# Interleaving the k products of the first two x chunks, with x1 loaded ahead of wk0 and the transposes and later loads held back

## The chip, the cores and the metric

The kernel runs on one core of one Trainium2 chip. The metric is the device time of one execution in microseconds (us), as a median over several executions. PE is the matrix engine, DVE the vector engine, ACT the scalar engine, SP the engine that issues most of the loads. To "turn" a chunk is to transpose it on PE, by products with an identity matrix. "SP's queue" and "ACT's queue" are the DMA issues of those two engines.

## The reference, cut to what matters

The whole computation is a gated mix of a linear-attention block and an MLP mixer over 2048 rows of 640 numbers. Only its first stage matters here: k = x @ wk, of which the rest of the attention block is made.

```python
qkv = (x @ wqkv) ...            # wqkv is 640 x 1920; its middle third is wk
phi = lambda t: jnp.where(t > 0, t + 1, jnp.exp(t)) + 1e-6
pq, pk = phi(q), phi(k)
g = sigmoid((x * gate_w).sum(-1, keepdims=True))   # the gate, computed as a 641st column of k
...                              # attention, mixer, g * a + (1 - g) * b
```

## The kernel before

x is cut into 16 chunks of 128 rows, wk into 5 pieces of 128 rows (160 KB each). A product for k needs x transposed (xT). Chunks 0 and 1 are loaded plain and turned on PE; chunks 2 to 15 are transposed by DMA. The issue order is: SP's queue x0, wk1, wk3, wk4, then the transposes; ACT's queue gate_w, wk0, x1, wk2.

```python
    load_x(0, 1)
    aq.dma_start(g5[:], gate_w.rearrange("(c p) -> c p", p=P))
    load_wk(sp, 1)
    load_wk(aq, 0)
    load_x(1, 2, aq)
    load_wk(sp, 3)
    load_wk(aq, 2)
    load_wk(sp, 4)
    for c0, c1 in ((2, 3), (3, 4), (4, 6), (6, 8), (8, 12), (12, 16)):
        load_xT(c0, c1)
    sp.dma_start(wq_sb, wqkv_v[:, :, 0:D])
    load_x(2, 8)
    load_x(8, 16)
    ...
```

The k products of one chunk are 5 pieces times 2 halves. A filler (`warmup`) is a product of ones that nobody reads; it only keeps PE busy.

```python
    def k_mm(pt, c, dcs, first=0, last=DC - 1):
        for dc in dcs:
            for hf in range(2):
                n = HD + hf
                nc.tensor.matmul(pt[:, hf, 0:n], lhsT=xT[:, dc, c * P:(c + 1) * P],
                                 rhs=wk_sb[:, dc, hf * HD:hf * HD + n], start=(dc == first), stop=(dc == last))

    warm = pair()
    one = nc.const_aps.tensor(1.0, (P, TS), BF16)

    def warmup(n, w=TS):
        for i in range(n):
            nc.tensor.matmul(warm[:, 1, 0:w], lhsT=one[:, 0:P], rhs=one[:, 0:w], start=True, stop=True)
    nc.vector.memset(g5z[:], 0.0)
    nc.vector.tensor_copy(g5z[0:DC, :], g5[:])
    warmup(5)
    warmup(1, 3 * P)
    kp = pair()
    turns = [(pair(), a, b) for a, b in ((0, 2), (2, DC))]

    def turn(c):
        for pt, a, b in turns:
            ptb = pt[:, 0, :].bitcast(BF16) if c else pt[:, 0, :]
            for dc in range(a, b):
                dst, src = ptb[:, (dc - a) * P:(dc - a + 1) * P], x_sb[:, c, dc * P:(dc + 1) * P]
                if c:
                    nc.tensor.transpose(dst, src, ident[:])
                else:
                    nc.tensor.matmul(dst, lhsT=src, rhs=ident[:], start=True, stop=True)
            if c == 0 and b == DC:
                nc.tensor.matmul(pt[:, 1, 0:DC], lhsT=g5z[:], rhs=ident[:, 0:DC], start=True, stop=True)
            nc.vector.tensor_copy(xT[:, a:b, c * P:(c + 1) * P],
                                  ptb[:, 0:(b - a) * P].rearrange("p (c s) -> p c s", c=b - a))
            if c == 0 and b == DC:
                nc.vector.tensor_copy(wk_sb[:, :, D], pt[:, 1, 0:DC])

    turn(0)
    warmup(1, TS)
    for n, dc in enumerate(k0_order):
        if n == 3:
            turn(1)
        elif 1 <= n < 3:
            warmup(1, 2 * P)
        k_mm(kp, 0, (dc,), first=k0_order[0], last=k0_order[-1])
    k_evac(kp, 0)
    for c in range(1, NCH):
        pt = pair()
        k_mm(pt, c, range(DC))
        k_evac(pt, c)
```

After k come q, the attention sums and the mixer, all of it PE work in program order, with nothing of the change in it.

## Time and profile before

| | before |
|---|---|
| median of 3 runs | 264.6 us (264.48 to 264.68) |
| span of the profiled run | 262.6 us |
| PE busy | 257.9 us, 98% |
| k chunk 2 starts | 8.35 us |
| k chunk 4 starts / its transpose landed | 11.07 / 9.72 us |
| k chunk 8 starts / its transpose landed | 16.52 / 16.44 us |
| first product of the next large group (`x_sb`,`pk`) | 49.01 us |

The landing times here and below are the times at which the last of the 16 partial signals of a load arrived, read from the trace. The starts are those of the 160 k products in order. These come from the packed traces product by product and signal by signal, and most of them stand in no view shown here.

First the page of before: the span, the busy line, the busy tenths of PE and of the DMA engines in 40 slices of 6.6 us, and the head of the chain that ended last.

```profile
span 262.6 us, 4246 instructions
...
PE 257.9 (98%) x1719; PEld 160.0 (61%) x1738; DVE 142.7 (54%) x282; ACT 82.7 (31%) x123; POOL 20.2 (8%) x65
...
PE   8999999999999999999999999999999999999995
...
DMA  7999987016682566600132000051100051100011
...
PE 98%; issue 0%; DVE 0%
```

PE is all that counts: its own work is 98% of the chain. Next, the chain in order of time in before, cut to the pieces from 4.69 to 27.6 us (start, length, what):

```profile
4.69 0.03 issue
4.72 0.43 PE pp L186
5.14 0.21 PE pp L199
5.36 0.47 PE pp L186 x2
5.83 0.11 PE pp L199
5.94 0.27 PE pp L186 x2
6.21 0.32 PE pp L214 x5
6.53 21.05 PE pp L186 x154
```

The one of these pieces that is not PE work is 30 ns of "issue" at 4.69 us (the second half of the first product has just been held up by the gate column); from there PE works on without a wait. The stretch from 3.2 us in windows, before (length, then busy time of PE, PE weight loads, DVE, ACT, POOL with counts, the granted clock, the DMA share, GB/s; the DMA share adds up the times of packets over 16 engines and can exceed 1):

```profile
3.20:6.00 2.80, 2.77 (x16) 1.67 (x15) 0.97 (x3) 0.82 (x1) 1.42 (x5) 1.00 1.14 336
6.00:8.30 2.30, 2.30 (x21) 1.69 (x20) 0.87 (x3) 0.77 (x2) 0.00 (x0) 1.00 1.16 233
```

PE is busy 2.77 of 2.80 us and then 2.30 of 2.30 us. The timeline of PE of before shows what it does (start, length, engine, line, operation, operands, shape, count):

```profile
5.15 0.68 PE L186 MATMUL pp<-wk_sb,xT 128*128 128x320 bf16 x2
5.66 0.27 PE L199 MATMUL pp<-const-bfloat16-1.0 128*128 128x256 bf16 x1
5.77 0.44 PE L186 MATMUL pp<-wk_sb,xT 128*128 128x320 bf16 x2
6.08 0.45 PE L214 MATMUL pp<-ident,x_sb 128*128 128x128 bf16 x5
6.44 5.75 PE L186 MATMUL pp<-wk_sb,xT 128*128 128x320 bf16 x41
```

A product of 320 columns follows the last after 267 ns up to about 5.6 us, and after 136 ns later. The Trainium skill, "TensorE: Matmul & The Clock Gate", Part 1, says that PE passes half of its clock pulses until it has been busy for a window of about 3.4 us, and that the moment varies between runs since the window runs free. This agrees: at the page's half rate of 1.2 GHz, 320 columns would take 267 ns (an estimate from its figure), and the trace has 267 ns. The granted clock reads 1.00 all the same, so it does not show this half rate; the spacing of the products does.

Last, the transposes in SP's timeline of before (start, length of issuing all six), and DVE's two copies of the first turn in its own timeline:

```profile
2.65 14.00 SPq L122 DMA_TRANSPOSE xT<-in_A_x_dram  x6
```

```profile
3.69 0.89 DVE L219 CAST xT<-pp 128x256 bf16<-128x256 f32 x2 [1.28 <-PE pp L216]
```

The transposes are issued from 2.65 us on. DVE's first copy starts at 3.69 us, released by the second turn product (L216).

### The profile page before, as it was taken

How to read it: one execution, taken by the hardware profiler on the slowest of the kernel's cores; microseconds unless marked ns; L12 is line 12 of the kernel's file. 1: busy time of each engine (PE TensorE's matmuls, PEld its weight loads, DVE VectorE, ACT ScalarE, POOL GpSimd, SP SyncE). 2: the span in 40 equal slices, each digit the busy share in tenths (PEclk: the TensorE clock that was granted, in tenths of full speed). 3: DMA queues.
4: the chain of work that ended last, by engine and by line, in shares of the span. 5: the costliest groups of instructions: out<-in, count | busy, mean ns of one | idle time of the engine just before them, and what ended most of it. 6: DMA issues, size and time to landing. Idle time of an engine off the chain costs nothing.

```text
span 262.6 us, 4246 instructions
## 1 busy us (share of the span) xinstructions
PE 257.9 (98%) x1719; PEld 160.0 (61%) x1738; DVE 142.7 (54%) x282; ACT 82.7 (31%) x123; POOL 20.2 (8%) x65
## 2 busy tenths in 40 slices
PE   8999999999999999999999999999999999999995
PEld 4777555788755644555577555567565577555553
DVE  2788778899947998955403464413356223112132
ACT  1555554321166236522502222412131332142200
POOL 5000050012210040001000001000001000000000
DMA  7999987016682566600132000051100051100011
GB/s 204 197 171 379 364 248 304 0 27 125 125 99 58 111 121 167 235 0 2 25 75 77 25 0 2 0 100 52 50 0 2 1 100 52 50 0 2 0 50 50
DMA packets 45757, 23.98 MB, mean 91 GB/s; under 512 B 35114, under 2 KB 44970, under 8 KB 45738
## 3 DMA queue, kind: packets, MB, share of 16 engines
q1 hardware_dynamic: 45296, 23.22, 35.1%
q10 hardware_dynamic: 442, 0.49, 0.5%
q8 instruction: 13, 0.21, 0.4%
q14 instruction: 6, 0.05, 0.1%
HBM read 12.21 MB, written 2.62 MB: 56 GB/s over the span
## 4 chain that ended last, share of the span: by engine, by line
PE 98%; issue 0%; DVE 0%
PE pp L500 22%; PE pp L467 21%; PE pp L186 9%; PE pp L315 8%; PE pp L451 8%; PE pp L420 8%; PE pp L349 8%; PE pp L243 8%; PE pp L199 1%; PE pp L387 1%; PE pp L475 1%; PE pp L509 1%; PE pp L368 1%; PE pp L258 0%; PE pp L216 0%
## 5 line engine op out<-in xcount | busy, mean ns | idle before, releaser
L467 PE MATMUL pp<-lnxT,w_sb 128*128 128x512 bf16 x249 | 59.8, 379 | 0.6
L500 PE MATMUL pp<-w_sb,h 128*128 128x384 bf16 (+3 forms) x414 | 57.6, 299 | 0.2 <-issue 0.2
L469 ACT ACTIVATE h<-pp 128x1024 bf16<-128x1024 f32 (+1 forms) x28 | 26.9, 961 | 82.2 <-PE pp L467 82.2
L500 PEld LDWEIGHTS <-h 128*128 128x128 bf16 x416 | 38.3, 98 | 19.3 <-issue 1.1
L467 PEld LDWEIGHTS <-w_sb 128*128 128x128 bf16 x260 | 25.4, 98 | 26.8
L514 DVE SCALAR_TENSOR_TENSOR oc<-pp,omg,x 128x640 bf16<-128x640 f32 (+2 forms) x20 | 14.4, 748 | 45.1 <-ACT h2x L478 21.3
L454 DVE SCALAR_TENSOR_TENSOR x<-pp,gate,x 128x640 f32<-128x640 f32 x16 | 13.9, 868 | 29.4 <-PE pp L451 29.4
L178 ACT ACTIVATE e<-pp 128x640 bf16<-128x640 f32 (+1 forms) x26 | 21.5, 826 | 9.6 <-PE pp L243 9.6
L451 PE MATMUL pp<-m_sb,pqT 128*128 128x320 bf16 x160 | 24.3, 299 | 0.0
L420 PE MATMUL pp<-w_sb,hsT 128*128 128x320 bf16 x160 | 23.9, 299 | 0.0
L423 DVE TENSOR_TENSOR x<-pp,x_sb 128x640 f32<-128x640 f32 x16 | 13.1, 820 | 19.7 <-PE pp L420 19.7
L186 PE MATMUL pp<-wk_sb,xT 128*128 128x320 bf16 (+1 forms) x160 | 23.1, 303 | 0.0
L315 PE MATMUL pp<-x_sb,pk 128*128 128x320 bf16 (+1 forms) x160 | 22.0, 300 | 0.0
L243 PE MATMUL pp<-xT,hsT 128*128 128x512 bf16 x98 | 21.6, 379 | 0.1
L315 PEld LDWEIGHTS <-pk 128*128 128x128 bf16 x160 | 18.8, 117 | 3.2
L420 PEld LDWEIGHTS <-hsT 128*128 128x128 bf16 x160 | 15.7, 98 | 8.2
L451 PEld LDWEIGHTS <-pqT 128*128 128x128 bf16 x160 | 15.7, 98 | 7.7
L186 PEld LDWEIGHTS <-xT 128*128 128x128 bf16 x160 | 15.7, 99 | 6.5 <-DVE xT L219 0.2
L349 PE MATMUL pp<-lnxT,w_sb 128*128 128x512 bf16 x76 | 17.9, 379 | 0.2
L243 PEld LDWEIGHTS <-hsT 128*128 128x128 bf16 x100 | 11.8, 118 | 9.7
L285 POOL TENSOR_SCALAR rstd<-mv 128x4 f32<-128x4 f32 (+1 forms) x11 | 3.4, 312 | 153.6 <-DVE mv L291 153.6
L180 DVE SCALAR_TENSOR_TENSOR pk<-pp,e 128x640 bf16<-128x640 f32 x16 | 13.2, 825 | 1.7
(76 smaller groups left out, 189.9 us busy)
## 6 DMA issues: line engine op xcount, KB each, us to landing
out_dram<-oc SPq DMA_DIRECT2D x14, 160.0 KB, 1.8
w_sb<-in_B_w_dram SPq DMA_DIRECT2D x1, 2160.0 KB, 8.4
w_sb<-in_B_w_dram SPq DMA_DIRECT2D x1, 2080.0 KB, 9.9
x_sb<-in_A_x_dram SPq DMA_DIRECT2D x1, 1280.0 KB
x_sb<-in_A_x_dram SPq DMA_DIRECT2D x1, 960.0 KB, 7.4
wo_sb<-in_A_wo_dram SPq DMA_DIRECT2D x6, 160.0 KB, 7.8
hsT<-in_A_wqkv_dram SPq DMA_DIRECT2D x1, 800.0 KB, 5.1
m_sb<-in_A_wqkv_dram SPq DMA_DIRECT2D x1, 800.0 KB, 12.0
```

Of the source, the lines that this page charges most:

```text
L178: nc.scalar.activation(ev, src, ACT.Exp)
L186: nc.tensor.matmul(pt[:, hf, 0:n], lhsT=xT[:, dc, c * P:(c + 1) * P], rhs=wk_sb[:, dc, hf * HD:hf * HD + n], start=(dc == first), stop=(dc ...
L243: nc.tensor.matmul(pt[:, t % 2, :], lhsT=wq_sb[:, dc, :].rearrange("p (m j) -> p j m", j=DC)[:, j], rhs=xT[:, dc, t * TS:(t + 1) * TS], st ...
L315: nc.tensor.matmul(pt[:, hf, 0:HD + hf], lhsT=w, rhs=x_sb[:, c, hf * HD:(hf + 1) * HD + hf], start=(c == 0), stop=(c == NCH - 1))
L349: nc.tensor.matmul(pt[:, i, :], lhsT=w, rhs=lnxT[t][:, dc, :], start=(dc == 0), stop=(dc == DC - 1))
L420: nc.tensor.matmul(pt[:, hf, 0:HD], lhsT=hsT[:, fc, 2 + c * P:2 + (c + 1) * P], rhs=w2_sb[:, fc, hf * HD:(hf + 1) * HD], start=(fc == 0), ...
L451: nc.tensor.matmul(pt[:, hf, 0:HD], lhsT=pqT[:, j, c * P:(c + 1) * P], rhs=m_sb[:, j, hf * HD:(hf + 1) * HD], start=(j == 0), stop=(j == D ...
L454: nc.vector.scalar_tensor_tensor(x1, pt[:, :, 0:HD], gate[:, c:c + 1], x1, op0=ALU.mult, op1=ALU.add)
L467: nc.tensor.matmul(pt[:, k, :], lhsT=w3_sb[:, dc, fc * P:(fc + 1) * P], rhs=lnT[:, dc, :], start=(dc == 0), stop=(dc == DC - 1))
L469: nc.scalar.activation(h2[:, 2 * i * TS:(2 * i + n) * TS], pt[:].rearrange("p h e -> p (h e)")[:, 0:n * TS], ACT.Gelu_apprx_tanh)
L500: nc.tensor.matmul(dst, lhsT=st[t]["h2"][:, fc * TS + cc * P:fc * TS + (cc + 1) * P], rhs=w4_sb[:, fc, a:b], start=start and fc == 0, stop ...
L514: nc.vector.scalar_tensor_tensor(oc[:, a:b], src, omg[:, c:c + 1], st[t]["x1"][cc][:, a:b], op0=ALU.mult, op1=ALU.add)
```

## The change

The intent: use each wk piece for both first chunks as soon as it lands, so that nothing of chunk 1 is left when the last piece has come. For this x1 is loaded ahead of wk0 on ACT's queue, chunk 1 is turned early by plain products, and ACT copies it out. The gate column is copied ahead of the larger copy. The transposes and everything behind them are held back by a memset on the first transposed column, so that they don't take DMA time from the wk pieces.

```diff
--- before.py
+++ after.py
@@ -127,24 +127,26 @@
     load_x(0, 1)
     aq.dma_start(g5[:], gate_w.rearrange("(c p) -> c p", p=P))
     load_wk(sp, 1)
-    load_wk(aq, 0)
     load_x(1, 2, aq)
     load_wk(sp, 3)
+    load_wk(aq, 0)
+    load_wk(sp, 4)
     load_wk(aq, 2)
-    load_wk(sp, 4)
-    for c0, c1 in ((2, 3), (3, 4), (4, 6), (6, 8), (8, 12), (12, 16)):
-        load_xT(c0, c1)
-    sp.dma_start(wq_sb, wqkv_v[:, :, 0:D])
-    load_x(2, 8)
-    load_x(8, 16)
-    sp.dma_start(wv_sb[:], wqkv_v[:, :, 2 * D:3 * D])
-    sp.dma_start(w1_sb[:], B_w1.rearrange("(c p) f -> p c f", p=P))
-    for g in range(NG):
-        sp.dma_start(wo_sb[:, g, :], A_wo[row0[g]:row0[g] + P, :])
-    for g in range(4):
-        sp.dma_start(w2_sb[:, g, :], B_w2[CG * g:CG * g + P, :])
-        sp.dma_start(w2_sb[32 * g:32 * (g + 1), 4, :], B_w2[CG * g + P:CG * (g + 1), :])
-    sp.dma_start(w3_sb[:], B_w3.rearrange("(c p) f -> p c f", p=P))
+
+    def late_loads():
+        for c0, c1 in ((2, 3), (3, 4), (4, 6), (6, 8), (8, 12), (12, 16)):
+            load_xT(c0, c1)
+        sp.dma_start(wq_sb, wqkv_v[:, :, 0:D])
+        load_x(2, 8)
+        load_x(8, 16)
+        sp.dma_start(wv_sb[:], wqkv_v[:, :, 2 * D:3 * D])
+        sp.dma_start(w1_sb[:], B_w1.rearrange("(c p) f -> p c f", p=P))
+        for g in range(NG):
+            sp.dma_start(wo_sb[:, g, :], A_wo[row0[g]:row0[g] + P, :])
+        for g in range(4):
+            sp.dma_start(w2_sb[:, g, :], B_w2[CG * g:CG * g + P, :])
+            sp.dma_start(w2_sb[32 * g:32 * (g + 1), 4, :], B_w2[CG * g + P:CG * (g + 1), :])
+        sp.dma_start(w3_sb[:], B_w3.rearrange("(c p) f -> p c f", p=P))
 
 
     nc.gpsimd.memset(mhalf[:], -0.5)
[cut: the copies of w1x are moved behind late_loads()]
@@ -190,47 +189,48 @@
         nc.scalar.copy(ylog[:, c:c + 1], pt[:, 1, HD:HD + 1])
         phi(pk[:, c, :].rearrange("p (h e) -> p h e", h=2), pt[:, :, 0:HD], D)
 
-    k0_order = (1, 0, 3, 4, 2)
     warm = pair()
     one = nc.const_aps.tensor(1.0, (P, TS), BF16)
 
-    def warmup(n, w=TS):
+    def warmup(n, w=TS, pt=warm):
         for i in range(n):
-            nc.tensor.matmul(warm[:, 1, 0:w], lhsT=one[:, 0:P], rhs=one[:, 0:w], start=True, stop=True)
+            nc.tensor.matmul(pt[:, 1, 0:w], lhsT=one[:, 0:P], rhs=one[:, 0:w], start=True, stop=True)
+
+    def turn(pt, c, copy, split):
+        for h, (a, b) in enumerate(((0, split), (split, DC))):
+            for dc in range(a, b):
+                nc.tensor.matmul(pt[:, h, (dc - a) * P:(dc - a + 1) * P], lhsT=x_sb[:, c, dc * P:(dc + 1) * P],
+                                 rhs=ident[:], start=True, stop=True)
+        if c == 0:
+            nc.tensor.matmul(pt[:, 0, 2 * P:2 * P + DC], lhsT=g5z[:], rhs=ident[:, 0:DC], start=True, stop=True)
+        for h, (a, b) in enumerate(((0, split), (split, DC))):
+            copy(xT[:, a:b, c * P:(c + 1) * P], pt[:, h, 0:(b - a) * P].rearrange("p (c s) -> p c s", c=b - a))
+            if c == 0 and h == 0:
+                copy(wk_sb[:, :, D], pt[:, 0, 2 * P:2 * P + DC])
 
     nc.vector.memset(g5z[:], 0.0)
     nc.vector.tensor_copy(g5z[0:DC, :], g5[:])
     warmup(5)
     warmup(1, 3 * P)
-    kp = pair()
-    turns = [(pair(), a, b) for a, b in ((0, 2), (2, DC))]
-
-    def turn(c):
-        for pt, a, b in turns:
-            ptb = pt[:, 0, :].bitcast(BF16) if c else pt[:, 0, :]
-            for dc in range(a, b):
-                dst, src = ptb[:, (dc - a) * P:(dc - a + 1) * P], x_sb[:, c, dc * P:(dc + 1) * P]
-                if c:
-                    nc.tensor.transpose(dst, src, ident[:])
-                else:
-                    nc.tensor.matmul(dst, lhsT=src, rhs=ident[:], start=True, stop=True)
-            if c == 0 and b == DC:
-                nc.tensor.matmul(pt[:, 1, 0:DC], lhsT=g5z[:], rhs=ident[:, 0:DC], start=True, stop=True)
-            nc.vector.tensor_copy(xT[:, a:b, c * P:(c + 1) * P],
-                                  ptb[:, 0:(b - a) * P].rearrange("p (c s) -> p c s", c=b - a))
-            if c == 0 and b == DC:
-                nc.vector.tensor_copy(wk_sb[:, :, D], pt[:, 1, 0:DC])
-
-    turn(0)
-    warmup(1, TS)
-    for n, dc in enumerate(k0_order):
-        if n == 3:
-            turn(1)
-        elif 1 <= n < 3:
-            warmup(1, 2 * P)
-        k_mm(kp, 0, (dc,), first=k0_order[0], last=k0_order[-1])
-    k_evac(kp, 0)
-    for c in range(1, NCH):
+    tp = pair()
+    turn(tp, 0, nc.vector.tensor_copy, 2)
+    nc.vector.memset(xT[:, 0:1, 2 * P:2 * P + 1], 0.0)
+    late_loads()
+    for dc in range(DC):
+        for g in range(4):
+            nc.gpsimd.tensor_copy(w1x[:, dc, 32 * g:32 * (g + 1)], w1_sb[:, dc, CG * g + P:CG * (g + 1)])
+    warmup(1, 3 * P)
+    kps = [pair(), pair()]
+    order = (1, 0, 3, 4, 2)
+    for n, (c, dc) in enumerate(((0, 1), (0, 0), (0, 3), (1, 1), (1, 0), (1, 3), (0, 4), (1, 4), (0, 2), (1, 2))):
+        if n == 1:
+            turn(warm, 1, nc.scalar.copy, 4)
+        if n in (1, 2):
+            warmup(1, 2 * P, kps[1])
+        k_mm(kps[c], c, (dc,), first=order[0], last=order[-1])
+    for c in range(2):
+        k_evac(kps[c], c)
+    for c in range(2, NCH):
         pt = pair()
         k_mm(pt, c, range(DC))
         k_evac(pt, c)
```

More of the change, by code (lines that the diff above doesn't have):

```diff
@@ L167 @@
         nc.gpsimd.memset(kvT[:, b:b + 2], 0.0)
-    for dc in range(DC):
-        for g in range(4):
-            nc.gpsimd.tensor_copy(w1x[:, dc, 32 * g:32 * (g + 1)], w1_sb[:, dc, CG * g + P:CG * (g + 1)])
     def phi(dst, src, n):
```

## The prediction

> **What bounds the kernel now.** The matrix engine (PE): the page's busy line gives it 257.9 of 262.6 us (98%), and the chain of waits is 98% PE. It works in program order almost without idle time, so the change pays what it moves the start of k chunk 2, and costs any wait that it makes later in the k stage.
>
> **The start, from the timeline and the landings of the loads.** x chunk 0 lands at 3.09 us, its turn runs 3.23 to 3.84, k chunk 0 begins at 4.22 (wk1 landed 4.17), stalls behind the gate column (second product at 4.72), then wk0, wk3 (5.33), x1 (6.03), wk4 (6.40), wk2 (6.58). k chunk 1 runs from 6.99, chunk 2 from 8.35; then 1.364 us a chunk, no gap. Products go at half rate up to about 5.64 us (320 columns: 267 ns apart against 136 later); the Trainium skill, "TensorE: Matmul & The Clock Gate", section on the HAM clock gate, describes such a half-rate start, and this trace agrees.
>
> **What the change does early.** Removed: chunk 1's ten products done in one block after all pieces (1.36 us), two fillers, the stall at the gate column (about 0.24 us, since its copy now comes before the large one). Added: chunk 1's ten products interleaved; its turn at about 4.75 in the half-rate time (5 x 107 ns instead of 5 x 56), copied out by ACT (my estimate from its 640- and 1024-column times: 0.9 us, hidden). x1 lands earlier, about 4.4, but wk0 takes x1's place in ACT's queue, so it lands at 5.5 to 6.0 instead of 4.36, and PE will wait for it after the turn. Then 18 products of 136 ns and a 107 ns filler remain. Chunk 2 would start at 8.1 if nothing waited, at 8.6 if wk0 lands at 6.0: my estimate 8.3. The loads bound this stretch, and their bytes are the same.
>
> **What holding back costs.** The transposes were issued from 2.65 but their packets start only at 5.3, behind the wk packets, so they hardly disturbed those. Now the first issue waits for vector copies and a memset, about 4.85; an isolated transpose of this trace takes 2.6 us, so chunk 2 lands at about 7.5 instead of 7.2, chunk 3 at 8.7 instead of 7.84, chunks 4-5 near 10.9 (9.72), needed near 11.0. Before, chunks 8-11 landed at 16.44 and were needed at 16.53: no slack, partly because an instruction fetch of 1.9 us at 13.7 held a DMA engine. A shift of 0.5 to 2 us there becomes a PE wait before chunk 8, in full; estimate 0.7 us, perhaps a little before chunk 4 or 6. Chunks 12-15 (18.67, needed 22.0), wq (21.8, needed 27.4) and later loads have slack.
>
> **Sum.** 264.6 - 0.1 + 0.7 = 265.2 us; range 264.2 to 266.6. Faster by over 2%: 0.01; within 2%: 0.97; slower: 0.02.
>
> **What would show it.** Right: chunk 2 begins within 0.3 us of 8.35; first transpose issue near 4.85; PE idle 0.3 to 2 us before chunk 8, released by the transpose; from q products on all is shifted by a constant. Wrong: no PE gap in the k stage (then 264.3 to 264.6), or chunk 2 well before 8.1.
>
> **What would make it wrong.** Transposes that catch up once no loads stand before them; an instruction fetch at another moment; wk0 landing at 5.3 or earlier; the full rate granted later because of idle PE in the start; the first vector copy waiting for the whole bank.

## The result

The changed kernel took 265.66 us (median of 6 runs, 265.21 to 266.90) against 264.45 us (6 runs, 264.15 to 264.68). The ratio is 1.0051 with a 95% interval of 1.0029 to 1.0072. Ratios here are the mean time of one kernel's runs over that of the other's of the same rounds, so they are not quite the ratio of the medians quoted. By the 2% rule this is "same"; by the interval it is half a per cent slower.

The page of after, in the same lines as before:

```profile
span 263.7 us, 4268 instructions
...
PE 259.0 (98%) x1738; PEld 159.9 (61%) x1738; DVE 141.7 (54%) x281; ACT 83.4 (32%) x125; POOL 20.2 (8%) x65
...
PE   7999999999999999999999999999999999999995
...
DMA  5899989015664456700132000051100042100011
...
PE 96%; DMA 2%; ACTq 0%; DVE 0%; issue 0%
```

PE's share is unchanged, but a DMA now holds 2% of the chain. The chain in order of time of after, from 1.78 to 28.7 us, says which:

```profile
1.78 4.81 DMA wk_sb<-in_A_wqkv_dram
6.59 0.04 issue
6.63 0.43 PE pp L185 x2
7.07 0.11 PE pp L197
7.17 10.44 PE pp L185 x76
17.62 0.04 issue
17.66 11.07 PE pp L185 x80
```

Time 1.78 to 6.59 us is the load of a wk piece (wk0, the third issue of ACT's queue). A short gap shows at 17.62 us. The waits of PE for DMAs from 3 to 30 us in after (us in total, times, longest):

```profile
PE pp L185 <- DMA wk_sb<-in_A_wqkv_dram: 1.0, 1, 1.0
PEld L185 <- DMA xT<-in_A_x_dram: 0.6, 2, 0.4
```

The windows of after, to be compared with those of before:

```profile
3.20:6.00 2.80, 2.27 (x16) 1.44 (x16) 0.97 (x4) 1.21 (x2) 1.39 (x5) 1.00 0.85 259
6.00:8.30 2.30, 1.67 (x13) 1.23 (x13) 0.00 (x0) 0.36 (x2) 0.00 (x0) 1.00 0.61 129
```

PE's busy time fell from 2.77 to 2.27 us in the first stretch and from 2.30 to 1.67 us in the second. The DMA share fell too, from 1.14 to 0.85 and from 1.16 to 0.61: the transposes no longer fill the engines, and the wk pieces did not land earlier for it. SP's transposes and DVE's first copy in after:

```profile
5.05 12.79 SPq L122 DMA_TRANSPOSE xT<-in_A_x_dram  x6
```

```profile
4.04 0.42 DVE L207 CAST xT<-pp 128x256 bf16<-128x256 f32 x1 [1.17 <-PE pp L205]
```

The first transpose is issued at 5.05 us (before 2.65). DVE's first copy starts at 4.04 us, not 3.69, because it is now released by the gate product (L205), the last of the turn.

The whole difference can be summed from the starts of the k products: chunk 2 starts at 9.19 us instead of 8.35 (+0.84). Before chunk 4 PE waits 0.08 us and before chunk 8 0.21 us beyond the usual step of 1.362. Together that is 1.13 us; the first `x_sb`,`pk` product is at 50.15 us instead of 49.01 (+1.14), and the spans differ by 1.1 us. Nothing after the k stage changed.

### The profile page after: what moved, and what is told of

It is laid out like the page before. It is cut to its first block, busy times and chain, and to the rows that moved or that the text cites. A ratio compares the mean times of both kernels' runs of the same rounds, so it can differ in the third digit from the quotient of the medians.

```text
span 263.7 us, 4268 instructions
## 1 busy us (share of the span) xinstructions
PE 259.0 (98%) x1738; PEld 159.9 (61%) x1738; DVE 141.7 (54%) x281; ACT 83.4 (32%) x125; POOL 20.2 (8%) x65
## 4 chain that ended last, share of the span: by engine, by line
PE 96%; DMA 2%; ACTq 0%; DVE 0%; issue 0%
PE pp L500 22%; PE pp L467 21%; PE pp L185 8%; PE pp L315 8%; PE pp L451 8%; PE pp L420 8%; PE pp L349 8%; PE pp L243 8%; DMA wk_sb<-in_A_wqkv_dram 2%; PE pp L387 1%; PE pp L475 1%; PE pp L509 1%; PE pp L368 1%; PE pp L258 0%; ACTq L128 0%; ACTq L119 0%
## 5 line engine op out<-in xcount | busy, mean ns | idle before, releaser
L467 PE MATMUL pp<-lnxT,w_sb 128*128 128x512 bf16 x260 | 60.4, 379 | 0.0
L349 PE MATMUL pp<-lnxT,w_sb 128*128 128x512 bf16 x80 | 18.1, 379 | 0.0
L178 DVE TENSOR_SCALAR e<-e 128x640 bf16<-128x640 bf16 (+1 forms) x26 | 9.5, 365 | 10.1 <-ACT e L177 9.1
## 6 DMA issues: line engine op xcount, KB each, us to landing
m_sb<-in_A_wqkv_dram SPq DMA_DIRECT2D x1, 800.0 KB, 12.1
```

Of the source, the lines that this page charges most:

```text
L349: nc.tensor.matmul(pt[:, i, :], lhsT=w, rhs=lnxT[t][:, dc, :], start=(dc == 0), stop=(dc == DC - 1))
L467: nc.tensor.matmul(pt[:, k, :], lhsT=w3_sb[:, dc, fc * P:(fc + 1) * P], rhs=lnT[:, dc, :], start=(dc == 0), stop=(dc == DC - 1))
```

## The experiments

All outputs are right. This table is what the traces say of the k stage. "Order" is the order of ACT's queue (old: wk0, x1, wk2; new: x1, wk0, wk2), "first issue" that of the first transpose. "Waits" are the steps between chunk starts beyond 1.362 us. Each row is one profile. The runs after the first result were made in three sets on three chips; the median of before was 264.34 or 264.35 us in each set.

| kernel | order | first issue | wk3 lands | 3rd of ACT lands | last piece lands | chunk 2 starts | chunk 4 lands | waits before chunk: us |
|---|---|---|---|---|---|---|---|---|
| before | old | 2.65 | 5.33 | 6.03 | 6.58 | 8.35 | 9.72 | none |
| before_again | old | 2.65 | 5.33 | 5.53 | 6.34 | 8.39 | 9.76 | none |
| hold_only | old | 4.72 | 5.29 | 5.53 | 6.67 | 8.40 | 11.54 | 4: 0.46 |
| after | new | 5.05 | 6.37 | 6.59 | 7.46 | 9.19 | 11.95 | 4: 0.08, 8: 0.21 |
| after_again | new | 5.07 | 5.96 | 6.14 | 7.00 | 8.93 | 11.98 | 4: 0.37, 8: 0.38 |
| wk3_first | new | 5.06 | 5.72 | 5.90 | 6.70 | 8.59 | 12.10 | 4: 0.82, 8: 0.17 |
| hold_shorter | new | 4.52 | 5.90 | 6.08 | 6.91 | 8.83 | 11.38 | 8: 0.14 |
| singles | new | 5.06 | 5.09 | 5.51 | 6.30 | 8.35 | 10.68 | 5: 0.38, 6: 0.88, 8: 1.08 |
| head_only | new | 2.65 | 6.51 | 6.70 | 7.64 | 10.91 | 10.40 | none |
| head_fill | new | 2.65 | 6.20 | 6.52 | 7.38 | 9.12 | 10.21 | none |
| swap_loads | new | 2.65 | 6.25 | 6.43 | 7.33 | 10.80 | 10.20 | none |
| candidate | new | 2.66 | 6.72 | 6.90 | 7.79 | 8.93 | 10.64 | none |
| candidate_held | new | 4.17 | 6.53 | 6.73 | 7.54 | 8.75 | 10.90 | none |

My theory after the result: there are two costs. The new head (load order and interleaving) makes PE wait for wk0, and the holding back makes the transposes late. They partly hide each other, since chunk 4 can't start before its transpose has landed, however late or early the head was. The rivals: the late wk0 was chance; the hold is the whole loss; the hold is free or even protects the loads. (A chunk 2 at 10.8 or 10.9 us in the table holds a second thing, PE at its slow rate; see head_only and swap_loads.)

### after_again: the changed kernel once more

> The changed kernel as it is, once more on the chip that runs the parts. In its first profile wk0 landed at 6.59 us, because 3 of the 16 partial landings came about 0.8 us after the other 13 (last of the 13 at 5.73). Theory 'queue place': wk0 is now the third load on ACT's queue and lands at 6.0 us or later in every profile; chunk 2 of k starts at 8.6 us or later, and the time is 0.8 to 1.4 us above before. Rival 'straggling by chance': wk0 lands at 5.5 to 5.8 this time, chunk 2 starts at about 8.3 us, and the time is within 0.6 us of before.

Measured: 265.61 us (265.47 to 265.86) against 264.34; ratio 1.0046 (1.0033 to 1.0059). wk0 landed at 6.14 us, chunk 2 started at 8.93 us. The loss repeats, and so does the late wk0; chance alone does not explain it.

### head_only: the new head, nothing held

```diff
     load_wk(aq, 2)
     def late_loads(): ...
+    late_loads()
 ...
-    nc.vector.memset(xT[:, 0:1, 2 * P:2 * P + 1], 0.0)
-    late_loads()
```

> The changed head (load order, early turn of chunk 1, interleaved products), but transposes and later loads issued at once as before. Theory 'two costs that overlap': the head alone costs what it moves the start of chunk 2, +0.3 to +0.9 us, and no wait for a transpose appears (chunks 8-11 land at 16.4 to 17, needed at about 17.4). Rival 'holding back is the whole loss': within 0.2 us of before, chunk 2 at about 8.3 us. Rival 'holding back protects the wk loads': wk0 and wk2 land later than in the changed kernel, and it is slower than the changed kernel.

Measured: 265.08 us, with a wide spread (264.56, 264.63, 264.80, 265.36, 265.50, 266.87); ratio 1.0034 (1.0010 to 1.0057). No wait for a transpose shows in its trace, so the head alone costs time, and "holding back is the whole loss" falls. The profile fell on the slowest run. Its PE timeline:

```profile
6.74 0.69 PE L186 MATMUL pp<-wk_sb,xT 128*128 128x320 bf16 x2 [0.75 <-DMA wk_sb<-in_A_wqkv_dram]
7.23 0.42 PE L198 MATMUL pp<-const-bfloat16-1.0 128*128 128x256 bf16 x1
7.44 4.73 PE L186 MATMUL pp<-wk_sb,xT 128*128 128x320 bf16 x24
```

The last line merges the 24 products that start before the window's end at 12 us; they take 4.73 us. Product by product in the trace, they follow each other after 267 ns until 9.85 us. In this run PE had not reached its full rate before it waited 0.75 us for wk0, and it got there at about 10.1 us, 4.5 us later than in before. The same work, from the first wk0 product to chunk 2, took 4.17 us here and 2.56 us in after, so about 1.6 us of this run's loss is the slow rate. So the head costs +0.2 to +1.2 us in five runs and 2.5 in one. The last rival, that it would be slower than the changed kernel because the hold protects the loads, was not met in the time; its last piece did land later, at 7.64 us.

### hold_only: the old head, transposes held

```diff
     turn(0)
+    nc.vector.memset(xT[:, 0:1, 2 * P:2 * P + 1], 0.0)
+    late_loads()
[cut: late_loads() is made of the same issues as in the change; the copies of w1x follow it]
     warmup(1, TS)
```

> The head of before, unchanged, but the transposes and later loads held back until the first turn is copied, by the same memset. Theory 'two costs that overlap': first transpose issue at about 4.9 us, chunk 2 still starts at 8.35 us, chunks 8-11 land at 17.2 to 17.8 us against a need at 16.5, so PE waits 0.7 to 1.3 us there, and the time is +0.8 to +1.4 us; the two parts alone then sum to more than the whole change. Rival 'holding back is free': within 0.2 us of before, wk4 and wk2 landing before 6.2 us.

Measured: 265.22 us (264.85 to 265.69) against 264.34; ratio 1.0032 (1.0020 to 1.0044). The waits of PE's weight loads from 7 to 30 us in hold_only (us in total, times, longest):

```profile
PEld L185 <- DMA xT<-in_A_x_dram: 0.6, 1, 0.6
```

In before the same view has no line at all. (It counts from the end of the last weight load, so its 0.6 us is a little more than the 0.46 us by which PE's step is longer.) The loss came as expected in size at +0.9 us in the medians (+0.5 in the profiled run, the fastest of its five), but in the wrong place: the wait is before chunk 4, whose pair of chunks landed at 11.54 us, and not before chunk 8. Chunks 8 to 11 landed at 16.44 us, exactly as in before. An instruction fetch of 16 KB held a DMA engine for 1.9 us from 13.7 us in before and for 1.2 us from 15.5 us in after, while those chunks were in flight; in hold_only it came at 18.4 us, when they had landed. That this fetch made the difference is not shown: in wk3_first it came at 19.4 us, also too late to matter, and the four chunks took 6.8 us from issue to landing against 5.8 in hold_only and 6.7 in after. With the old order, holding back made the pieces no earlier: the last landed at 6.67 us, against 6.58 and 6.34 not held.

The two parts alone sum to +1.6 us in the medians (0.74 + 0.88), the whole change is +1.27 in the same rounds. This is what the theory of overlap says, but the intervals of the three ratios are too wide to show a difference of 0.35 us; the overlap is read from the traces, in the next run.

### wk3_first: only the order of the products

```diff
-((0, 1), (0, 0), (0, 3), (1, 1), (1, 0), (1, 3), (0, 4), (1, 4), (0, 2), (1, 2))
+((0, 1), (0, 3), (1, 1), (1, 3), (0, 0), (1, 0), (0, 4), (1, 4), (0, 2), (1, 2))
```

> The changed kernel with one edit: the order of the interleaved products, wk3 for both chunks ahead of wk0. Theory 'the wait is for wk0 itself': the first product after the turn starts when wk3 lands (5.4 to 6.4 us), chunk 2 starts 0.2 to 0.5 us earlier than in the changed kernel of the same rounds, but the time falls by less than that, since chunk 8 must still wait for its transpose until about 17.6 us (0.0 to 0.3 us faster than the changed kernel). Rival 'all the last loads are late alike': no difference.

Measured: 265.53 us (265.28 to 266.64); ratio 1.0054 (1.0037 to 1.0071). Chunk 2 started at 8.59 us, 0.34 earlier than in after_again, and the time did not fall: the wait before chunk 4 grew from 0.37 to 0.82 us, because its transpose landed at 12.10 us all the same. The waits of PE's weight loads for transposes from 7 to 30 us, first in after_again and then in wk3_first:

```profile
PEld L185 <- DMA xT<-in_A_x_dram: 1.1, 2, 0.6
PEld L185 <- DMA xT<-in_A_x_dram: 1.3, 2, 1.0
```

This is the clearest sight of the overlap. The hold pins chunk 4 at 12.0 to 12.1 us (11.07 in before), and a better head is handed back there. In the three profiles with this hold and pair (after, after_again, wk3_first) the head's delay was 0.84, 0.58 and 0.24 us, the waits for transposes 0.29, 0.75 and 0.99, and the sums 1.13, 1.33 and 1.23.

### swap_loads: only the order of two loads, in the kernel before

```diff
-    load_wk(aq, 0)
     load_x(1, 2, aq)
+    load_wk(aq, 0)
     load_wk(sp, 3)
```

> The kernel before with one edit: on ACT's queue x chunk 1 is loaded ahead of wk0, nothing else. In the four profiles with the changed load order the third loads (wk3, wk0) landed at 5.7 to 6.5 and 5.9 to 6.7 us and the last at 6.7 to 7.6; in the two with the order of before at 5.3 and 5.5 to 6.0 (x1), the last at 6.6 to 6.7. Theory 'the order itself makes wk0 late, and pieces with it': wk0 at 5.8 to 6.7, wk3 at 5.7 or later, chunk 2 of k at 8.6 us or later, time +0.2 to +0.8 us. Rival 'the early turn or the held transposes delay the loads': wk3 lands at 5.3 and the last piece by 6.7 as in before; time within 0.2 us.

Measured: 266.78 us (265.27, 266.77, 266.79, 266.92) against 264.35; ratio 1.0076 (1.0048 to 1.0103). PE's timeline in swap_loads:

```profile
4.93 0.42 PE L199 MATMUL pp<-const-bfloat16-1.0 128*128 128x256 bf16 x1
6.47 0.70 PE L186 MATMUL pp<-wk_sb,xT 128*128 128x320 bf16 x2 [1.11 <-DMA wk_sb<-in_A_wqkv_dram]
```

The landings are as expected; the time is not, at +2.4 us in the median instead of +0.2 to +0.8 (one run of four is at +0.9). PE waits 1.11 us for wk0, and after it works at the slow rate until about 9.6 us. Of the 2.45 us by which chunk 2 is late, 1.32 are the later start of the wk0 products (6.47 instead of 5.15 us), and 1.13 the slower work after it. In the two profiles in which PE stood idle for 0.75 us or more before it had its full rate (head_only and this one), that rate came at 10.1 and 9.6 us; in the other eleven it was there by 6.6 us, in after by 5.24, ahead of its wait. That is a pattern in the profiles and no experiment.

wk3 landed at 6.25 us although its own issue did not move, and the last piece at 7.33. One swap of two issues of the same size is enough, in this profile. In the three profiles with the old order wk3 landed at 5.29 to 5.33 us; in the ten with the new order at 5.09 to 6.72, nine of them at 5.72 or later. In the changed kernel's first profile 13 of the 16 partial signals of wk0 were there by 5.73 us and the other three came at 6.50 to 6.59. The Trainium skill, "DMA: Bandwidth & Descriptors", section "Why a DMA increments its semaphore by 16 and not by 1", says that the engines of one DMA finish independently and that only the full count means that all has landed; this trace agrees, and the last engines cost 0.86 us. Single late signals are not confined to the new order: in before, x1 in the same third place had 13 signals by 5.32 us and the last at 6.03, where they held PE up by only about 0.03 us. Why some engines fall behind, and more so in the new order, is not shown by any run.

### head_fill: more filler in the wait for wk0

```diff
-            warmup(1, 2 * P, kps[1])
+            warmup(4 if n == 1 else 1, TS if n == 1 else 2 * P, kps[1])
```

> The changed head without holding back (as in head_only), with four filler products of 512 columns in place of one of 256 in the wait for wk0. Theory 'the slow runs of head_only (up to 266.9 us; its profile shows products 267 ns apart until 9.6 us) come from idle time on PE, which puts off the full rate': the filler removes them, all runs lie between 264.3 and 265.6 us, products are 136 ns apart from 7 us at the latest. Rival 'the late full rate is chance': one or more of the runs above 266 us again. The fillers themselves cost 0 to 0.4 us when wk0 lands early.

Measured on head_only with this edit: 265.18 us (264.58, 264.76, 265.08, 265.28, 265.35, 267.34); ratio 1.0039 (1.0006 to 1.0072). Five runs lie in the expected range, one at 267.34 us does not, so the filler did not remove the slow runs, though the theory said it would. The profile cannot test the theory either: its full rate was there by 4.53 us, before the added filler began at 5.09. The slow run has no trace of its own, so whether it had a late full rate is open.

### singles: chunks 4 and 5 as two transposes

```diff
-        for c0, c1 in ((2, 3), (3, 4), (4, 6), (6, 8), (8, 12), (12, 16)):
+        for c0, c1 in ((2, 3), (3, 4), (4, 5), (5, 6), (6, 8), (8, 12), (12, 16)):
```

> The changed kernel with one edit: the transpose of chunks 4 and 5 issued as two of one chunk. With a pair, chunk 4 landed 4.2 us after its issue in every held kernel (11.5 to 12.1 us), and k chunk 4 started just then (11.6 to 12.1, before: 11.07). Theory 'the pair pins chunk 4': chunk 4 lands at 10.3 to 10.8 us, there is no wait before it, and what was waited for there (0.1 to 0.8 us) is waited for later or saved: time 0 to 0.4 us below the changed kernel, with a longer wait before chunk 8, because chunks 8-11 are issued about 1 us later. Rival 'the transposes are bound by what they move': chunk 4 lands at 11.5 us or later.

Measured: 266.94 us (266.76 to 267.09); ratio 1.0094 (1.0073 to 1.0115), 1.3 us above the changed kernel's 265.61 of the earlier rounds (before: 264.34 and 264.35 in the two) and not a little below it. The waits of PE's weight loads in singles:

```profile
PEld L185 <- DMA xT<-in_A_x_dram: 2.8, 3, 1.2
```

The mechanism was right for chunk 4: it landed at 10.68 us, and chunk 4 started at 11.08 with no wait. The saving was wrong: every further issue costs SP's queue about 1.3 us, chunk 5 landed at 12.77, chunks 6 and 7 at 15.01, chunks 8 to 11 at 18.83, and PE waited for each. This run is also the one where the new order landed well (wk0 at 5.51 us), and even then chunk 2 started at 8.35 us, which is where before starts it.

### hold_shorter: the hold ended after the first copy

```diff
             copy(xT[:, a:b, c * P:(c + 1) * P], ...)            # first copy of the first turn
             if c == 0 and h == 0:
+                nc.vector.memset(xT[:, 0:1, 2 * P:2 * P + 1], 0.0)
                 copy(wk_sb[:, :, D], ...)
 ...
-    nc.vector.memset(xT[:, 0:1, 2 * P:2 * P + 1], 0.0)
     late_loads()
```

> The changed kernel with the memset that ends the hold moved from behind the three copies of the first turn to behind the first one, about 0.5 us earlier. Theory 'the first issue sets when chunk 4 can start': first issue at about 4.5 us (5.05), chunk 4 lands at 11.3 to 11.6 us (11.95), which is before its need of 11.66 to 11.92, so the wait before chunk 4 is at most 0.2 us and the time is 0.2 to 0.5 us below the changed kernel's 265.61. Rival 'chunk 4 lands late for another reason (what the transposes move, or the loads ahead of them)': lands at 11.8 us or later, time as the changed kernel.

Measured: 265.21 us (264.89 to 265.25) against 264.34; ratio 1.0029 (1.0016 to 1.0041), 0.4 us below after_again's 265.61. The first issue moved by 0.53 us (5.05 to 4.52) and chunk 4's landing by 0.57 us (11.95 to 11.38). The wait before chunk 4 is gone, and 0.14 us before chunk 8 is left. The moment of the first issue does set when chunk 4 lands: in the six held profiles that transpose chunks 4 and 5 as a pair, it landed 6.7 to 7.0 us after the first issue.

### candidate and candidate_held: tries to beat both

The candidate is head_only with the first turn in two tiles, chunk 1's copies on DVE and ACT side by side, other filler, and this order of products. The held one ends the hold after the first copy.

```diff
-    turn(warm, 1, nc.scalar.copy, 4)
+    turn((warm, tp), 1, (nc.vector.tensor_copy, nc.scalar.copy), 3)
 ...
+((0, 1), (1, 1), (0, 3), (1, 3), (0, 0), (1, 0), (0, 4), (1, 4), (0, 2), (1, 2))
```

> A try to beat both: nothing held back, x1 early as in the change, the first turn in two tiles again so that its first copy waits for its own products only, the turn of chunk 1 copied by DVE and ACT side by side, wk1 and wk3 products of both chunks ahead of wk0, filler in the waits. Theory 'the head loses only by the order of its waits': first k product at 4.2 us, chunk 2 starts at 8.0 to 8.4 us, no wait for a transpose, time 264.0 to 264.5 us, 0 to 0.4 us below before. Rival 'the loads bound it, the last piece lands late in this order': chunk 2 at 8.5 us or later, 264.5 to 265.3 us.

Measured: 264.70 us (263.87 to 265.47) against 264.35; ratio 1.0008 (0.9986 to 1.0029). This is no gain that the runs can show, and the time and chunk 2 at 8.93 us both lie where the rival had put them. The two tiles did bring DVE's first copy back to 3.69 us. PE's timeline of the candidate:

```profile
5.70 0.45 PE L186 MATMUL pp<-wk_sb,xT 128*128 128x320 bf16 x2 [0.33 <-DVE xT L208]
6.76 5.47 PE L186 MATMUL pp<-wk_sb,xT 128*128 128x320 bf16 x39 [0.61 <-DMA wk_sb<-in_A_wqkv_dram]
```

It still waits 0.33 us for chunk 1's copies and 0.61 us for wk3, which landed at 6.72 us.

> The candidate of the last runs (264.70 us, its profile: wk3 6.72, wk0 6.90, last piece 7.79 us) with the transposes held, but only to the end of the first copy, about 4.2 us. In the new load order the last piece landed at 6.3 to 7.5 us in four held profiles and at 7.3 to 7.8 in four that were not held. Theory 'in this order, holding back does protect the loads': last piece at 6.3 to 7.4 us, wk3 before 6.4; chunk 2 at 8.0 to 8.7; a wait before chunk 4 of at most 0.3 us (lands at about 11.1); time 264.0 to 264.8. Rival 'no protection': last piece at 7.3 us or later, time 264.8 to 265.5.

Measured: 264.82 us (264.73 to 264.88); ratio 1.0018 (1.0005 to 1.0030). The last piece landed at 7.54 us, wk3 at 6.53 and chunk 2 started at 8.75, all outside what the theory of protection allowed; the last piece and the time are as the rival said. Over all profiles with the new order the last piece landed at 6.30 to 7.54 us when held (six) and at 7.33 to 7.79 us when not (four), so a small protection is possible in this order, but no run isolates it. In candidate_held no wait for a transpose is left, and its time is still no better than the candidate's.

### before_again: the kernel before once more

> The kernel before as it is, for a second profile of its load order without holding back, beside one held profile. Theory 'the order sets how late the last pieces land': wk3 at 5.4 us or earlier, the last piece by 6.8 us, chunk 2 of k at 8.35 to 8.5 us, chunk 8 with a wait of at most 0.3 us. Rival 'chance': wk3 at 5.7 us or later, or the last piece at 7 us or later. Ratio 1.000 within its interval.

Measured: 264.32 us (264.23 to 264.89); ratio 1.0005 (0.9989 to 1.0020). wk3 landed at 5.33 us, the last piece at 6.34, chunk 2 started at 8.39, with no wait before chunk 8. The old order behaves alike in its three profiles.

## Why the prediction was right or wrong

The predicted time was 265.2 us in a range of 264.2 to 266.6; measured were 265.66 and 265.61 us. The direction of the whole and the mechanism of both terms (a wait for wk0, a wait for transposes) hold. The sizes did not, and the early term had the wrong sign; the measured loss of 1.2 us is twice the forecast 0.6, inside a range that was wide enough.

- "bounds the kernel now": right. PE was 98% of the chain, and a shift in the k stage went through to the end in full (+1.13 us summed in the k stage, +1.14 at 49 us, +1.1 in the spans).
- "What the change does early", chunk 2 at 8.3 us: this step failed. The term was sized at -0.1 us; it measured +0.84 and +0.58 us in the two profiles. The prediction named the reason, wk0 in x1's place on ACT's queue, but let it land at 5.5 to 6.0 us like x1 before; it landed at 6.59 and 6.14. With these landings its own sum (8.6 us for a landing at 6.0) gives 9.19 and 8.74 us, and 9.19 and 8.93 were measured; the 0.19 us in after_again is two products at the slow rate (218 and 244 ns instead of 136). So the landing was the wrong figure, and not the sum. swap_loads shows wk0, wk3 and the last piece late by the order alone, in its one profile; over all profiles the new order did so in nine of ten. The words "The loads bound this stretch, and their bytes are the same" were too simple: the bytes were the same and the landings were not.
- One cost in the list of risks came true: the first vector copy waited for the whole turn (4.04 instead of 3.69 us), and the first k product started at 4.53 instead of 4.22 us. In after it is hidden behind the wait for wk0.
- The first issue "about 4.85": 5.05 us, and the turn of chunk 1 "at about 4.75": 5.04 us, both late by that same delay. ACT's copies, estimated at 0.9 us and hidden, ran from 5.61 to 6.36 us, before wk0 had landed: right.
- "a PE wait before chunk 8, in full; estimate 0.7 us": the term measured 0.29 us in one profile and 0.75 in the other, but from a quarter (after) to all (hold_only) of it sat before chunk 4. The prediction let chunks 4-5 land near 10.9 us from a 2.6 us isolated transpose (one inside the chip's memory). From HBM, chunk 2 took 3.4 us, chunk 3 took 2.9 us and the pair 4.2 us from issue to landing, so chunk 4 landed at 11.95 us. It took 4.4 us in before too. In singles, with the same issues ahead of it, chunk 4 alone took 3.0 us, so it is the pair that made it long.
- In after the two misses partly cancel (+0.94 and -0.41 us), in after_again they do not (+0.68 and +0.05). This is no accident: a late head uses up the wait for the transposes, so the more the head loses, the less of the hold's cost is left to see.
- "From q products on all is shifted by a constant": right.
- Why there was nothing to gain: in before PE was busy 2.30 of 2.30 us while the last pieces landed. The number of k products did not change, so interleaving could only save fillers and the stall at the gate column. singles is the nearest to a best case in the runs: landings early, chunk 2 at 8.35 us, no better than before, though its first k product was late (4.53 us).

Open: why the new load order lets single DMA engines fall behind; whether the hold protects the loads a little in that order; and what sets the runs near 267 us in head_fill.

## What to carry to other kernels

Before rearranging work to use data as it lands, look at how much idle time and filler the engine has in that stretch; here it had 0.03 us of idle time in 5.1 us, and 0.7 us of filler. When two parts of a change delay the same stage, measure each alone: the later wait hides the earlier one, and curing one of them gives nothing until the other is cured too. A load's landing is that of its slowest engine, so swapping two loads of equal size is a change to be measured, and not a neutral step.

## What the Trainium skill lacked or had wrong

- "DMA: Bandwidth & Descriptors", section "DMA Transpose (X-bar)": it has no time from issue to landing by size (elsewhere the page has an effective bandwidth of transposes, but not this). Here, from HBM, one chunk of 128 x 640 took 2.9 us (chunk 3 in after), a pair 4.2, four chunks 5.8 (hold_only) to 7.9 (before, with more queued ahead); from on-chip memory one block of 128 x 640 took 2.6 us. Splitting a pair into two issues cost about 1.3 us of the queue's time for the added one.
- The same page tells that the engines of a DMA finish independently, not how far apart: here the last signal of a 160 KB load came up to 1.7 us after the 13th (wk3 in candidate, 5.02 and 6.72 us), and the order of two equal loads on one queue moved the landing of a third on another queue by 0.9 us (wk3, 5.33 to 6.25, one profile of swap_loads).
- "TensorE: Matmul & The Clock Gate", Part 1: the half rate agrees (267 and 136 ns for 320 columns). The variation is wider than the page has it: it puts the full rate at around 4 us of sustained work, give or take 500 ns, and here, where PE had worked without a gap of more than 0.03 us since its first product at 0.83 us, that rate came 2.7 us (candidate) to 5.1 us (hold_only) after that product. What it doesn't have is the size of the tail after a short idle time: the full rate came at about 5.6 us in before and at about 10.1 us in head_only, where PE had waited 0.75 us before reaching it; that profile is of a run 1.8 us above the median of its kernel.
